# Loading a weight matrix with one 128-partition transfer per slice, three later loads in flight, and a randomly shaken schedule

## Chip, cores, metric

The kernel runs on one core of a Trainium2 chip. The metric is device time in microseconds (us) per execution. The span in a profile, first to last instruction, is 1.7 to 1.9 us shorter than the measured time in nearly all runs. PE is the matmul engine, PEld its weight load, DVE the vector engine, ACT the scalar engine, POOL the general one, and SP the one that mostly issues transfers. ACT issues transfers too. "SPq" and "ACTq" are the instruction queues of SP and ACT. A transfer "lands" at its last completion event.

## The reference

```python
x = A_x                                   # 2048 x 448, bfloat16
xn = layernorm(x)
# branch A: linear attention, 16 heads of 28, feature map softmax(+/- q w_phi)
# branch B: the one that this change touches
h = silu(xn @ B_w1)                       # B_w1: 448 x 1792
branch_B = h @ B_w2                       # B_w2: 1792 x 448
return x + branch_A(xn) + branch_B
```

## The kernel before

The kernel is one program of about 4,900 instructions. A small list scheduler written in Python orders the instructions of each engine before they are emitted. PE's order is fixed by the program text; the scheduler only orders the other engines.

PE works on two halves of its rows at once: partitions 0 to 63 (`LO`) and 64 to 127 (`HI`). The 448 rows of w1 are seven slices `s` of 64 rows. In SBUF, `LO` holds columns 0 to 895 of a slice and `HI` holds columns 896 to 1791 of the same 64 rows. A pair of transfers, one issued by SP and one by ACT, brings in one or two slices. Both sides of each transfer have the 64 rows outermost:

```python
w1v = B_w1.rearrange("(s p) f -> p s f", p=64)
def load_w1(a, b, after=None):
    n = (b - a) * 64 * 896 * 2
    load(w1_sb[LO, a:b, :], w1v[:, a:b, 0:896],    n, 1792, f"w1l{a}", issue=480)
    load(w1_sb[HI, a:b, :], w1v[:, a:b, 896:1792], n, 1792, f"w1h{a}", eng="act", issue=480, after=after)
...
load_x(0, 1); load_x(1, 2)
load_w1(0, 2, after=...); load_w1(2, 4)
load_x(2, 3); load_x(3, 4, eng="act")
load_w1(4, 6); load_w1(6, 7)
```

PE starts with warm-up matmuls, transposes the first normalised tiles of x, and then needs slices 0 and 1, slices 2 and 3, and slices 4 to 6, in that order:

```python
f1a(0, 0, 2)                # tile 0, slices 0 and 1
X_tr(1, ...); X_ev(1, ...)  # transposes on PE, evictions on ACT and DVE
f1a(0, 2, 4); ...; f1a(1, 0, 4)
for h in range(2):          # then slices 4..6
    for s in range(4, NS): ...
```

The later loads (q/k weights, v weights, more of x, w2) each wait for a mark on PE's progress, so that they do not come too early.

The softmax here doesn't subtract the row's maximum and nothing guards it: scores larger than these inputs give would overflow.

Of the kernel before, what the change touches and what calls it, by code (L numbers as in the profile page):

```python
# [138 lines left out]
class _Prog:  # L139
# [56 lines left out]
            return 230.0  # L196
        return 110.0

    def schedule(self, pe0, passes=6):
        ops = self.ops  # L200
        for o in ops:
            for d in o.deps:
                ops[d].users.append(o.id)
            for d in o.odeps:
                assert ops[d].eng == o.eng, "order-only deps must be same-engine"
                ops[d].users.append(o.id)
        t = 0.0
        when = {}
        seen = False
        for o in ops:  # L210
            if o.eng == "pe":
                if o.name != "warm" and not seen:
                    seen = True
                    t = max(t, pe0)
                when[o.id] = t
                t += o.dur
        best = None
        for _ in range(passes):
            order, span = self._pass(when)
            if best is None or span < best[0]:  # L220
                best = (span, order, [(o.start, o.end) for o in ops])
            when = {oid: ops[oid].start for oid in order["pe"]}
        for o, (a, b) in zip(ops, best[2]):
            o.start, o.end = a, b
        self.order = best[1]
        self.makespan = best[0]
        return best[1]

    def _pass(self, when):
        ops = self.ops  # L230
        n = len(ops)
        lat = self.lat
        tend = max(when.values()) + 3000.0
        for o in reversed(ops):
            if o.eng == "pe":
                o.alap = when[o.id]
                continue
            m = tend
            for u in o.users:
                uu = ops[u]  # L240
                if u in o.odeps:
                    continue
                m = min(m, uu.alap - (lat(o, uu) if o.id in uu.deps else 0.0))
            extra = 0.0
            if o.is_dma:
                extra = o.fixed if o.fixed is not None else 1200.0 + o.nbytes
            o.alap = m - o.dur - extra

        ndeps = [len(o.deps) + len(o.odeps) for o in ops]
        ready = {e: set() for e in ENGINES}  # L250
        for o in ops:
            if ndeps[o.id] == 0:
                ready[o.eng].add(o.id)
        eng_free = {"pe": 800.0, "act": 800.0, "dve": 800.0, "pool": 800.0, "sp": 800.0}
        act_table = [None]
        dma_free = [0.0]
        order = {e: [] for e in ENGINES}
        done = 0
        WAIT_TOL = 60.0

        def est(o):
            t = eng_free[o.eng]
            for d in o.deps:
                dd = ops[d]
                t = max(t, dd.end + lat(dd, o))
            for d in o.odeps:
                t = max(t, ops[d].end if not ops[d].is_dma else ops[d].start + ops[d].dur)
            if o.eng == "act" and o.table is not None and act_table[0] is not None and o.table != act_table[0]:
                t += 1300.0
            return t  # L270

        while done < n:
            best = None
            for e in ENGINES:
                if not ready[e]:
                    continue
                c = [(est(ops[i]), ops[i]) for i in ready[e]]
                t0 = min(x[0] for x in c)
                t, o = min(((t, o) for t, o in c if t <= t0 + WAIT_TOL), key=lambda x: (x[1].alap, x[1].id))
                for t2, o2 in c:  # L280
                    if o2 is o or o2.alap >= o.alap or t2 >= t + o.dur:
                        continue
                    la = max(t - o.alap, t + o.dur - o2.alap, 0.0)
                    lb = max(t2 - o2.alap, t2 + o2.dur - o.alap, 0.0)
                    if lb < la - 1.0:
                        t, o = t2, o2
                if best is None or t < best[0]:
                    best = (t, o)
            assert best is not None, "scheduler deadlock"
            t, o = best  # L290
            ready[o.eng].discard(o.id)
            o.start = t
            if o.is_dma:
                issue_end = t + o.dur
                eng_free[o.eng] = issue_end
                if o.fixed is not None:
                    o.end = t + o.fixed
                else:
                    x0 = max(issue_end + 900.0, dma_free[0])
                    dma_free[0] = x0 + o.nbytes  # L300
                    o.end = dma_free[0] + 300.0
            else:
                o.end = t + o.dur
                eng_free[o.eng] = o.end + (0.0 if o.eng == "pe" else 30.0)
                if o.eng == "act" and o.table is not None:
                    act_table[0] = o.table
            order[o.eng].append(o.id)
            done += 1
            for u in o.users:
                ndeps[u] -= 1  # L310
                if ndeps[u] == 0:
                    ready[ops[u].eng].add(u)
        return order, max(o.end for o in ops)


def bass_parallel_sum__linear_kernel_hedgehog__dense_activation_silu__prompt_kernel(
# [16 lines left out]
    NB = 4  # L333
# [4 lines left out]
    with es:  # L338
# [68 lines left out]
        P = _Prog()  # L407
# [79 lines left out]
            load(x_sb[:, t0:t1, :], xv[:, t0:t1, :], (t1 - t0) * 128 * D * 2, (t1 - t0) * D * 2, f"x{t0}", issue=430, after=after,  # L487
                 eng=eng)

        w1v = B_w1.rearrange("(s p) f -> p s f", p=64)  # L490
        def load_w1(a, b, after=None):
            n = (b - a) * 64 * 896 * 2
            load(w1_sb[LO, a:b, :], w1v[:, a:b, 0:896], n, 1792, f"w1l{a}", issue=480)
            load(w1_sb[HI, a:b, :], w1v[:, a:b, 896:1792], n, 1792, f"w1h{a}", eng="act", issue=480, after=after)

        P.op("act", 1, lambda e: e.activation(tabw[:], neghalf[:], ACTF.Silu), [neghalf[:]], [tabw[:]],  # L496
             table="silu", name="tab", ordered=True)
        load_x(0, 1)
        load_x(1, 2)
        load_w1(0, 2, after=P.ops[P.last[("pool", "o")]])  # L500
        load_w1(2, 4)
        load_x(2, 3)
        load_x(3, 4, eng="act")
        load_w1(4, 6)
        load_w1(6, 7)
        P.op("pool", 300, lambda e: e.memset(BD[:], 0.0), [], [BD[:]], name="bd0", ordered=True)
        for p0 in (0, 904):
            P.op("pool", 150, lambda e, p0=p0: e.memset(wraw[:, :, p0:p0 + 8], 0.0), [], [wraw[:, :, p0:p0 + 8]],
# [1 line left out]
        wpv = A_w_phi.rearrange("(k q l) d f -> q l d k f", q=2, l=2)  # L510
        wvv = A_wqkv[:, 2 * D:3 * D].rearrange("(s p) c -> p s c", p=64)

        def load_wqk(after):
            load(wraw[:, 0:2, 8:904], A_wqkv[0:256, 0:896].rearrange("(b p) c -> p b c", p=128), 256 * 896 * 2, 1792, "wqk0",
                 after=after)
            load(wraw[:, 2, 8:904], A_wqkv[256:384, 0:896], 128 * 896 * 2, 1792, "wqk1", after=after)
            load(wraw[LO, 3, 8:904], A_wqkv[384:448, 0:896], 64 * 896 * 2, 1792, "wqk2", after=after)
            for q in range(2):
                for l in range(2):
                    p0 = (64 if q else 8) + l * DH  # L520
                    load(BD[p0:p0 + DH, :, l * DH:(l + 1) * DH], wpv[q, l], DH * NB * DH * 2, DH * 2, f"wphi{q}{l}", issue=430)

        w2v = B_w2.rearrange("(f p) d -> p f d", p=128)
        wov = A_wo.rearrange("(h s e) c -> s h e c", s=NS, e=4)
# [68 lines left out]
        def F1(c, i, j0, nt, mid=None):  # L593
# [3 lines left out]
            for s in range(NS):  # L597
                pair([(bank(2 * sl + q)[:, 0:n], w1_sb[HALF[q], s, i * 128:(i + 1) * 128],
                       xT[HALF[q], c % NXC, s, j0 * 128:j0 * 128 + n], s == 0, s == NS - 1) for q in range(2)], n, "f1")
                if mid is not None and s == 2:  # L600
                    mid()
            src = two(sl)[:, :, 0:n]
            dst = hT[:, c % NH, i:i + FH + 1:FH, j0 * 128:j0 * 128 + n]
# [218 lines left out]
                    F1mm(sa[u // 2], u % 2, u, s, t, 1)  # L822

        f1a(0, 0, 2)
        load_wqk(mark())
        X_tr(1, 3, 0, HS)
        X_ev(1, 3, 0, HS)
        f1a(0, 2, 4)
# [5 lines left out]
        LN_b(2, od=True)  # L834
        LN_b(3, od=True)
        pads_init()
        marks = [mark()]
        f1a(1, 0, 4)
        marks.append(mark())
        P.unit = "F1A"  # L840
        for h in range(2):
            for s in range(4, NS):
                for u in range(2):
                    F1mm(sa[h], u, 2 * h + u, s, 0, 2)
            F1silu(sa[h], 2 * h)
        marks.append(mark())
        sb_ = take()
        for u in range(2):
            P.unit = "F1B%d" % u
# [3 lines left out]
                X_tr(2, 3, 0, NS)  # L853
                X_ev(2, 3, both=True)
        F1silu(sb_, 4)
        marks.append(mark())
        sl = take()
        X_tr(3, sl, 0, NS)
        X_ev(3, sl, both=True)
        give(sl)  # L860
        F1(0, 6, 0, 2)
        marks.append(mark())
        FT_tr(0)
        for i in range(FH):
            F1(0, i, 2, 2)
            marks.append(mark())
            if i == 2:
                FT_tr(1)
            if i in (4, 5, 6):
                FM(i - 4)  # L870
        load(wv_sb[LO], wvv, D * D * 2, D * 2, "wv0", after=marks[2])
        load(wv_sb[HI], wvv, D * D * 2, D * 2, "wv1", after=marks[3])
        load_x(4, 6, after=marks[4])
        load(w2_sb[:, 0:7], w2v[:, 0:7], FF * D, 896, "w2", after=marks[5])
        load_x(6, 8, after=marks[7])
        load(w2_sb[:, 7:14], w2v[:, 7:14], FF * D, 896, "w2", after=marks[8])

        def prep(t):
            LN(t)
            X_dma(t)  # L880
# [188 lines left out]
```

## Time and profile before

| | before |
|---|---|
| median time of the first three runs | 152.81 us (152.14 to 152.93) |
| span of the profiled execution | 151.6 us |
| PE busy | 142.8 us, 94% of the span |
| w1 in all | 1.6 MB, 896 pieces of 1792 bytes |

The first view is part 2 of the page of the kernel before: the span in 40 slices of 3.8 us, busy share in tenths. PEclk is the clock granted to PE (time before the first clock event counts as full), and DMA is the mean busy share of the sixteen DMA engines. Shares of DMA add up packet times, so they can pass 1.

```profile
PE   6769959999999999999999999999999999999990
...
PEclk9959999999999999999999999999999999999999
DMA  3996895093772997239781023333376344863323
```

PE is full from the seventh slice on. Only the first 22 us have gaps, and there the DMA share is 0.84.

The chain of waits of the kernel before, in order of time (start, length, what), shows how small the gaps are:

```profile
2.49 6.10 DMA w_sb<-in_B_w_dram
...
8.73 1.04 PE psum L432 x16
...
12.07 1.81 PE psum L432 x30
...
20.71 1.57 issue
22.28 125.66 PE psum L432 x1774
...
147.96 0.62 DVE x_sb L752
```

From 22.28 us PE works for 125.66 us without a wait, and then the last addition and store follow. The early part is a wait for a w1 transfer. The 30 matmuls at 12.07 us begin with slice 6, the last, whose second half landed at 11.93 us. The piece called "issue" is 1.57 us in which PE stood still.

PE's waits of the kernel before (engine, line, what it waited for: total us, times, longest) name the same two:

```profile
PE psum L432 <- DMA w_sb<-in_B_w_dram: 2.1, 2, 1.3
PE psum L432 <- issue: 1.6, 1, 1.6
```

The DMA view of the kernel before lists the issues (what, queue, how many, KB each, median us from issue to landing). The w_phi load has no landing time. The view takes a landing from sixteen completion events, and the trace has only fifteen for each of these four small transfers of 28 rows:

```profile
w_sb<-in_B_w_dram SPq DMA_DIRECT2D x3, 224.0 KB, 5.4
w_sb<-in_B_w_dram ACTq DMA_DIRECT2D x3, 224.0 KB, 6.1
...
BD<-in_A_w_phi_dram SPq DMA_DIRECT2D x4, 6.1 KB
```

Two lines of PE's timeline before (start, length, what, count, idle before) show the clock. The same 16 matmuls of 128 columns take 0.62 us at full clock and 1.04 us after the second gap:

```profile
6.67 0.62 PE L432 MATMUL psum<-xT,w_sb 64*128 64x128 bf16 x16 [0.74 <-DMA w_sb<-in_B_w_dram]
...
8.73 1.04 PE L432 MATMUL psum<-xT,w_sb 64*128 64x128 bf16 x16 [1.32 <-DMA w_sb<-in_B_w_dram]
```

### The profile page before, as it was taken

To read this page: it belongs to the slowest core of one execution; us is meant where nothing else is said; L and a number is where in the kernel's file an instruction comes from. 1 tells how busy PE (TensorE), PEld (TensorE's weight loads), DVE (VectorE), ACT (ScalarE), POOL (GpSimd) and SP (SyncE) were. 2 spreads that over 40 slices of the span, in tenths; PEclk is the share of its full clock that TensorE was granted. 3 is DMA by queue.
4 is the path that set the end of the run, shared out by engine and by line. 5 is a ranking of instruction groups with operands and counts; after the bars stand their busy time and mean duration, and the time that the engine had idled before them with its cause. 6 is when DMAs were issued, how large, how long until landed. Compare 5 with 4: busy or idle time off the path is not lost.

```text
span 151.6 us, 4915 instructions
## 1 busy us (share of the span) xinstructions
PE 142.8 (94%) x2118; PEld 88.3 (58%) x2118; DVE 96.7 (64%) x179; ACT 84.4 (56%) x106; POOL 83.9 (55%) x95
## 2 busy tenths in 40 slices
PE   6769959999999999999999999999999999999990
PEld 2379957555556555555555556565556666666550
DVE  2747548699998376990129697874047694848633
ACT  3115748988955976895779587678573102011110
POOL 3307000706999996969902899999991402222130
PEclk9959999999999999999999999999999999999999
DMA  3996895093772997239781023333376344863323
GB/s 79 255 272 178 227 316 206 4 169 73 225 93 42 137 173 153 69 97 157 158 183 35 0 63 80 69 74 69 73 107 79 81 123 124 49 191 73 102 84 121
DMA packets 43678, 18.42 MB, mean 122 GB/s; under 512 B 36680, under 2 KB 43400, under 8 KB 43656
## 3 DMA queue, kind: packets, MB, share of 16 engines
q1 hardware_dynamic: 43000, 17.19, 53.6%
q10 hardware_dynamic: 656, 0.92, 2.4%
q8 instruction: 17, 0.28, 0.8%
q14 instruction: 5, 0.04, 0.1%
HBM read 7.48 MB, written 1.84 MB: 61 GB/s over the span
## 4 chain that ended last, share of the span: by engine, by line
PE 91%; DMA 4%; issue 1%; ACT 1%; DVE 0%; DVEq 0%; ACTq 0%
PE psum L432 90%; DMA w_sb<-in_B_w_dram 4%; PE psum L445 1%; ACT L496 1%; DVE x_sb L752 0%; DVEq L1020 0%; ACTq L463 0%
## 5 line engine op out<-in xcount | busy, mean ns | idle before, releaser
L640 POOL TENSOR_TENSOR E<-E,Rk 128x896 bf16<-128x896 bf16 x32 | 53.3, 1699 | 8.7 <-ACT E L450 6.3
L432 PE MATMUL psum<-xT,w_sb 64*128 64x512 bf16 (+2 forms) x522 | 48.1, 331 | 2.1 <-DMA w_sb<-in_B_w_dram 2.1
L432 PE MATMUL psum<-w_sb,hT 64*128 64x448 bf16 x448 | 45.2, 349 | 0.0
L450 ACT ACTIVATE hT<-psum 128x1024 bf16<-128x1024 f32 (+1 forms) x32 | 28.9, 917 | 12.8 <-PE psum L432 12.0
L432 PEld LDWEIGHTS psum<-xT,w_sb 64*128 64x128 bf16 x522 | 26.5, 98 | 15.4 <-DMA w_sb<-in_B_w_dram 1.7
L432 PEld LDWEIGHTS psum<-w_sb,hT 64*128 64x128 bf16 x448 | 24.1, 94 | 16.6
L633 DVE TENSOR_REDUCE Sk<-E 128x64 f32<-128x1792 bf16 x16 | 31.9, 2004 | 2.4 <-ACT E L450 2.3
L450 ACT ACTIVATE E<-psum 128x896 bf16<-128x896 f32 x32 | 27.4, 916 | 6.2 <-PE psum L432 6.0
L450 ACT ACTIVATE xT<-psum 128x448 f32<-128x448 f32 (+2 forms) x12 | 5.7, 481 | 33.8 <-PE psum L432 21.9
L432 PE MATMUL psum<-wqk,xT 64*128 64x448 bf16 x224 | 23.6, 349 | 0.0
L704 POOL TENSOR_TENSOR xT<-xT,x_sb 128x448 f32<-128x448 f32 x8 | 8.3, 1034 | 24.9 <-ACT xT L450 24.9
L432 PEld LDWEIGHTS psum<-wqk,xT 64*128 64x128 bf16 x224 | 12.2, 94 | 8.6
L557 DVE TENSOR_SCALAR xnd<-x_sb,mv,rstd 128x896 bf16<-128x896 bf16 (+2 forms) x18 | 11.1, 656 | 9.1 <-POOL rstd L547 9.1
L547 POOL TENSOR_TENSOR rstd<-ve,neghalf 128x1 f32<-128x1 f32 x16 | 8.8, 564 | 8.7 <-DVE ve L545 8.4
L692 POOL TENSOR_TENSOR Ye<-Ye,x_sb 128x448 f32<-128x448 f32 x8 | 8.2, 1035 | 7.7 <-DVE Ye L690 7.7
L432 PE MATMUL psum<-wv_sb,xT 64*128 64x448 bf16 x112 | 11.9, 349 | 0.0
L539 DVE BATCH_NORM_STATS2 st<-x_sb 128x6 f32<-128x448 bf16 x16 | 9.5, 608 | 3.4 <-DMA x_sb<-in_A_x_dram 3.4
L432 PE MATMUL psum<-wo_sb,E 64*128 64x448 bf16 x112 | 11.3, 349 | 0.0
L690 DVE TENSOR_TENSOR Ye<-psum,Ye 128x448 f32<-128x448 f32 x8 | 5.0, 621 | 9.0 <-ACT Ye L450 8.9
L729 DVE TENSOR_TENSOR E<-psum,rden 128x224 bf16<-128x224 f32 x32 | 10.3, 383 | 0.3
L545 POOL TENSOR_SCALAR ve<-mv 128x1 f32<-128x1 f32 x12 | 2.3, 216 | 12.4 <-DVE mv L543 12.4
L432 PEld LDWEIGHTS psum<-wo_sb,E 64*128 64x128 bf16 x112 | 6.2, 94 | 4.4
(42 smaller groups left out, 102.0 us busy)
## 6 DMA issues: line engine op xcount, KB each, us to landing
out_dram<-x_sb SPq DMA_DIRECT2D x8, 224.0 KB, 2.2
w_sb<-in_B_w_dram SPq DMA_DIRECT2D x2, 784.0 KB, 6.7
x_sb<-in_A_x_dram SPq DMA_DIRECT2D x2, 448.0 KB, 4.5
wv_sb<-in_A_wqkv_dram SPq DMA_DIRECT2D x2, 392.0 KB, 4.7
wo_sb<-in_A_wo_dram SPq DMA_DIRECT2D x14, 56.0 KB, 2.2
w_sb<-in_B_w_dram SPq DMA_DIRECT2D x3, 224.0 KB, 5.4
w_sb<-in_B_w_dram ACTq DMA_DIRECT2D x3, 224.0 KB, 6.1
phT<-in_A_wqkv_dram SPq DMA_DIRECT2D x1, 448.0 KB, 5.6
```

Of the source, the lines that this page charges most:

```text
L432: ins = e.matmul(dst, lhsT, rhs, start=st, stop=sp, skip_group_check=True)
L450: return P.op("act", d_act(n), lambda e: e.activation(dst, src, func, scale=scale), reads=reads or [src], writes=writes or [dst], table=ta ...
L539: P.op("dve", 630, lambda e: e.bn_stats(st6[:, t, :], xs), [xs], [st6[:, t, :]], name="bnst", ordered=od)
L545: lambda e: e.tensor_scalar(ve[:, t:t + 1], mv[:, t, 1:2], EPS_LN, None, ALU.add),
L547: P.op("pool", 580, lambda e: e.tensor_tensor(rstd[:, t:t + 1], ve[:, t:t + 1], neghalf[:], ALU.pow), [ve[:, t:t + 1], neghalf[:]], [rstd[ ...
L557: lambda e, dst=dst, src=src: e.tensor_scalar(dst, src, mv[:, t, 0:1], rstd[:, t:t + 1], ALU.subtract, ALU.mult),
L633: dve(lambda e: e.tensor_reduce(Sk[:, t % 3, :].rearrange("p (h g) -> p h g", g=2), Er, AXL.X, ALU.add), d_dve(1792), [Er], [Sk[:, t % 3, ...
L640: pool(lambda e, Eh=Eh, Rb=Rb: e.tensor_tensor(Eh, Eh, Rb, ALU.mult), 1770, [Eh, Rh], [Eh], "phi%d" % qk)
L690: dve(lambda e: e.tensor_tensor(y, b, y, ALU.add), d_dve(D), [b, y], [y], "ye_d")
L692: pool(lambda e: e.tensor_tensor(y, y, x_sb[:, t, :], ALU.add), 1110, [y, x_sb[:, t, :]], [y], "ye_x")
L704: pool(lambda e: e.tensor_tensor(y, y, x_sb[:, t, :], ALU.add), 1110, [y, x_sb[:, t, :]], [y], "yl_x")
L729: dve(lambda e, dst=dst, src=src, rb=rb: e.tensor_tensor(dst, src, rb, ALU.mult), d_dve(224), [src, r], [dst], "o")
```

## The change

The intent is to bring each w1 slice into all 128 partitions with one transfer, so that a slice is complete sooner and fewer transfers are issued. The later loads no longer wait for PE's progress. Each waits for the load three before it in a chain, and the w2 loads are cut in two. The list scheduler repeats its pass 400 times with random priorities and keeps the order with the shortest modelled time. The last lines of the diff ("early U" in the texts below) insert some matmuls of the attention branch two slices earlier into a late loop of branch B. The core of the diff:

```diff
-        w1v = B_w1.rearrange("(s p) f -> p s f", p=64)
-        def load_w1(a, b, after=None):
-            n = (b - a) * 64 * 896 * 2
-            load(w1_sb[LO, a:b, :], w1v[:, a:b, 0:896], n, 1792, f"w1l{a}", issue=480)
-            load(w1_sb[HI, a:b, :], w1v[:, a:b, 896:1792], n, 1792, f"w1h{a}", eng="act", issue=480, after=after)
+        w1v = B_w1.rearrange("(s p) (h f) -> h p s f", p=64, h=2)
+        chain = []
+        def chained(*args, **kw):
+            chain.append(load(*args, after=chain[-3], **kw))
+        def load_w1(a, b):
+            for s in range(a, b):
+                chain.append(load(w1_sb[:, s, :], w1v[:, :, s, :], 128 * 896 * 2, 1792, f"w1{s}", eng=("sp", "act")[s % 2], issue=480))
...
         load_x(0, 1)
-        load_x(1, 2)
-        load_w1(0, 2, after=P.ops[P.last[("pool", "o")]])
-        load_w1(2, 4)
-        load_x(2, 3)
+        load_x(1, 2, eng="act")
+        load_w1(0, 5)
+        load_x(2, 3, eng="act")
         load_x(3, 4, eng="act")
-        load_w1(4, 6)
-        load_w1(6, 7)
+        load_w1(5, 7)
...  (wqk, wv, x 4..7 and w2 go through chained(); the marks on PE's progress are gone)
-    def schedule(self, pe0, passes=6):
+    def schedule(self, pe0, passes=6, shaken=400):
...
+            if shake > 0 and not o.is_dma:
+                seed = (seed * 1103515245 + 12345) % 2147483648
+                o.alap += (seed / 2147483648.0 - 0.5) * 200.0 * (1 + shake % 5)
...
-                if mid is not None and s == 2:
+                if mid is not None and s == 0:
                     mid()
```

More of the change, by code (lines that the diff above doesn't have):

```diff
@@ L217, in schedule @@
         best = None
-        for _ in range(passes):
-            order, span = self._pass(when)
+        base = when
+        for k in range(passes + shaken):
+            if k == passes:
+                base = {oid: best[2][oid][0] for oid in best[1]["pe"]}
+            order, span = self._pass(base, k - passes + 1)
             if best is None or span < best[0]:
                 best = (span, order, [(o.start, o.end) for o in ops])
-            when = {oid: ops[oid].start for oid in order["pe"]}
+                if k >= passes:
+                    base = {oid: ops[oid].start for oid in order["pe"]}
+            if k < passes:
+                base = {oid: ops[oid].start for oid in order["pe"]}
         for o, (a, b) in zip(ops, best[2]):
@@ L227, in schedule, with _pass @@
         return best[1]
-    def _pass(self, when):
+    def _pass(self, when, shake=0):
         ops = self.ops
@@ L233, in _pass @@
         tend = max(when.values()) + 3000.0
+        seed = 7919 * max(shake, 0) + 17
         for o in reversed(ops):
@@ L511, in bass_parallel_sum__linear_kernel_hedgehog__dense_activation_silu__prompt_kernel, with load_bulk @@
         wvv = A_wqkv[:, 2 * D:3 * D].rearrange("(s p) c -> p s c", p=64)
-        def load_wqk(after):
-            load(wraw[:, 0:2, 8:904], A_wqkv[0:256, 0:896].rearrange("(b p) c -> p b c", p=128), 256 * 896 * 2, 1792, "wqk0",
-                 after=after)
-            load(wraw[:, 2, 8:904], A_wqkv[256:384, 0:896], 128 * 896 * 2, 1792, "wqk1", after=after)
-            load(wraw[LO, 3, 8:904], A_wqkv[384:448, 0:896], 64 * 896 * 2, 1792, "wqk2", after=after)
+        def load_bulk():
+            for b in range(NB):
+                r = 128 if b < 3 else 64
+                chained(wraw[0:r, b, 8:904], A_wqkv[b * 128:b * 128 + r, 0:896], r * 1792, 1792, f"wqk{b}", issue=450)
             for q in range(2):
@@ L521, in load_wqk @@
                     load(BD[p0:p0 + DH, :, l * DH:(l + 1) * DH], wpv[q, l], DH * NB * DH * 2, DH * 2, f"wphi{q}{l}", issue=430)
+            for q in range(2):
+                chained(wv_sb[HALF[q]], wvv, D * D * 2, D * 2, f"wv{q}")
+            chained(x_sb[:, 4:6, :], xv[:, 4:6, :], 256 * D * 2, 4 * D, "x4", issue=430)
+            for a, b in ((0, 4), (4, 7)):
+                chained(w2_sb[:, a:b], w2v[:, a:b], (b - a) * 128 * D * 2, D * 2, "w2", issue=430)
+            chained(x_sb[:, 6:8, :], xv[:, 6:8, :], 256 * D * 2, 4 * D, "x6", issue=430)
+            for a, b in ((7, 11), (11, 14)):
+                chained(w2_sb[:, a:b], w2v[:, a:b], (b - a) * 128 * D * 2, D * 2, "w2", issue=430)
         w2v = B_w2.rearrange("(f p) d -> p f d", p=128)
@@ L824, in bass_parallel_sum__linear_kernel_hedgehog__dense_activation_silu__prompt_kernel @@
         f1a(0, 0, 2)
-        load_wqk(mark())
+        load_bulk()
         X_tr(1, 3, 0, HS)
@@ L836, in bass_parallel_sum__linear_kernel_hedgehog__dense_activation_silu__prompt_kernel @@
         pads_init()
-        marks = [mark()]
         f1a(1, 0, 4)
-        marks.append(mark())
         P.unit = "F1A"
@@ L845, in bass_parallel_sum__linear_kernel_hedgehog__dense_activation_silu__prompt_kernel @@
             F1silu(sa[h], 2 * h)
-        marks.append(mark())
         sb_ = take()
@@ L855, in bass_parallel_sum__linear_kernel_hedgehog__dense_activation_silu__prompt_kernel @@
         F1silu(sb_, 4)
-        marks.append(mark())
         sl = take()
@@ L861, in bass_parallel_sum__linear_kernel_hedgehog__dense_activation_silu__prompt_kernel @@
         F1(0, 6, 0, 2)
-        marks.append(mark())
         FT_tr(0)
@@ L865, in bass_parallel_sum__linear_kernel_hedgehog__dense_activation_silu__prompt_kernel @@
             F1(0, i, 2, 2)
-            marks.append(mark())
             if i == 2:
@@ L870, in bass_parallel_sum__linear_kernel_hedgehog__dense_activation_silu__prompt_kernel @@
                 FM(i - 4)
-        load(wv_sb[LO], wvv, D * D * 2, D * 2, "wv0", after=marks[2])
-        load(wv_sb[HI], wvv, D * D * 2, D * 2, "wv1", after=marks[3])
-        load_x(4, 6, after=marks[4])
-        load(w2_sb[:, 0:7], w2v[:, 0:7], FF * D, 896, "w2", after=marks[5])
-        load_x(6, 8, after=marks[7])
-        load(w2_sb[:, 7:14], w2v[:, 7:14], FF * D, 896, "w2", after=marks[8])
         def prep(t):
```

## The prediction

> **What bounds the kernel now.** PE. The page gives PE 142.8 of 151.6 us busy. In the chain of waits the piece from 22.28 to 147.94 us is unbroken PE work (125.7 us, no wait); the tail (last addition, store) is 3.6 us. So only the first 22 us can give anything. There, by the timeline: PE waits 0.7 us and 1.3 us for w1 slices (until 6.67 and 8.73); the windows view shows a granted clock of 0.59 from 8.73 to 12.07, costing about 1.4 us; the last w1 piece lands at 11.9, just as PE wants it (12.04); and PE stands still from 20.71 to 22.28 ("issue", 1.6 us; a 16 KB instruction packet was still moving until 20.98 through DMA engines that were fully busy). The most that a perfect change could win is about 5 us; a realistic k=16 version of this one would win 1 to 3 us. The random shaking and the earlier insertion of U act where PE already never waits: worth nothing, at most harm.
>
> **What the change does to w1.** Bytes are the same (1.6 MB). Before, each transfer has 64 rows outermost on both sides, and each leaves 16 completion events in the trace. After, the source of a slice is [h=2][p=64][896 elements] and the destination is [128][896]. The Trainium skill (DMA: Bandwidth & Descriptors, "Why a DMA increments its semaphore by 16 and not by 1", on how many engines) says that a transfer is split over the largest k up to 16 that divides the outermost size of both sides. Here that is gcd(2, 128) = 2. This trace agrees with the rule where it can be tested: the four w_phi loads, 28 rows outermost, leave 15 events, as k = 14 plus one made-up remainder would; the others leave 16. So I expect the w1 load on two DMA engines instead of sixteen.
>
> **Cost.** In the trace a 1792-byte packet takes 75 to 79 ns of an engine at its best (and 100 to 120 when all sixteen are saturated). Two engines must each move 7 x 64 = 448 of them: 34 to 35 us, plus about 2.5 us for their share of x and the first wqk pieces, plus 2 us of start and 1 us of landing: slice 6 lands at about 39 to 40 us instead of 11.9. PE's order is fixed by the program, so it cannot work ahead. From the moment slice 6 is there, PE still has 147.96 - 12.07 - 1.57 = 134.3 us to do, about 1.7 us more because its clock will have dropped in the wait, then 3.6 us of tail and 1.2 us between span and measured time: 180 us. The loads chained behind w1 (wqk, wv, w2) start late too, but at 16 engines they should stay ahead of PE.
>
> **Prediction: 179 us.** The chance that the two-engine reading is right I put at about two in three: a tuned kernel's author would have noticed 30 us. If it is wrong, about 150.5 us. So the range has to be wide: 149 to 188. Chances: faster by over 2% 0.13, within 2% 0.21, slower 0.66.
>
> **What would show it.** Right: w1 issue-to-landing of 10 us and more, each w1 transfer with about 3 completion events, DMA share near 2/16 in the first 30 us, PE idle in stretches of about 10 us waiting for w1 by line, then unbroken work. Wrong: sixteen events per slice, slices landing 1 us apart, PE's two early waits shorter, clock at 1.0 from 9 to 12 us, and the 20.7 us gap gone or moved.
>
> **What would make it wrong.** The source's two outer sizes being merged or reordered before they reach the hardware; two engines running faster per packet than 75 ns; a new PE stall later from the shaken order.

## The result

| | before | after |
|---|---|---|
| median time | 152.87 us (152.14 to 152.98, 4 runs) | 178.88 us (178.72 to 179.89, 4 runs) |
| ratio after/before | | 1.171, 95% interval 1.165 to 1.178 |
| span of the profiled execution | 151.6 us | 177.0 us |
| last w1 piece landed | 11.9 us | 37.0 us |
| completion events per w1 transfer | 16 | 3 |
| median length of a 1792-byte packet, whole execution | 79 ns | 74 ns |
| the same, from 1 to 37 us | 100 ns | 74 ns |

Ratios and intervals are from fast runs alone, so they are not quite the ratio of the quoted medians.

The page of the kernel after, part 2 (slices of 4.4 us):

```profile
PE   6403151069999999999999999999999999999991
...
PEclk9965555558999999999999999999999999999999
DMA  2122111256975749039539880052228934383332
```

In the first eight slices PE is mostly idle, and so are the DMA engines: the kernel waits for a load while nearly all of the DMA engines are free. The windows view gives one stretch of that (start:end, length, busy us of PE, PEld, DVE, ACT and POOL, clock, DMA share, GB/s):

```profile
15.00:25.00 10.00, 2.36 (x46) 1.85 (x46) 0.32 (x2) 0.42 (x2) 0.00 (x0) 0.50 0.13 50
```

The DMA share is 0.13, about 2/16, and 50 GB/s are moved. Two engines that take 74 ns for 1792 bytes would move 48 GB/s (an estimate from these packets). Transfers of both SP and ACT were in flight then, so the two queues used the same two engines: spreading the slices over two queues did not spread them over more engines. The x loads show it too. They run on all sixteen, and of the first one behind w1 fourteen events came by 13.4 us and the last two only at 24.8 and 25.1 us. Before, the stretch from 8.04 to 11.45 us moved 269 GB/s.

The chain of waits after has two new pieces: SP's long issue of slice 4, and the 28 us from the start of slice 6's issue (8.9 us of them the issue itself) to its landing. The unbroken PE work that follows is as long as before:

```profile
2.55 6.33 SPq L473
...
8.92 28.12 DMA w_sb<-in_B_w_dram
...
37.08 3.38 PE psum L442 x29
...
47.77 125.63 PE psum L442 x1772
...
173.42 0.62 DVE x_sb L772
```

PE's waits after:

```profile
PE psum L442 <- DMA w_sb<-in_B_w_dram: 16.9, 5, 5.4
PE psum L442 <- ACT xT L460: 8.3, 1, 8.3
```

The first line was expected. The second one (8.3 us) was not: PE waited for ACT to evict the first transposed tile. The DMA view after shows that the w1 transfers have lost their landing time, just as the 28-row loads had none before, and that the three small x loads on ACT took 14.3 us from issue to landing (median):

```profile
w_sb<-in_B_w_dram SPq DMA_DIRECT2D x4, 224.0 KB
...
w_sb<-in_B_w_dram ACTq DMA_DIRECT2D x3, 224.0 KB
...
x_sb<-in_A_x_dram ACTq DMA_DIRECT2D x3, 112.0 KB, 14.3
```

Lines of the timeline after show why ACT was late:

```profile
1.25 16.54 SPq L473 DMA_DIRECT2D w_sb<-in_B_w_dram  x4
...
3.25 9.50 ACTq L473 DMA_DIRECT2D x_sb<-in_A_x_dram  x2
...
13.95 0.60 ACT L460 ACTIVATE xT<-psum 128x256 bf16<-128x256 bf16 x2 [11.66 <-issue]
...
14.48 1.22 PE L442 MATMUL psum<-xT,w_sb 64*128 64x128 bf16 x16 [8.26 <-ACT xT L460]
...
21.33 0.61 PE L442 MATMUL psum<-xT,w_sb 64*128 64x128 bf16 x8 [5.42 <-DMA w_sb<-in_B_w_dram]
...
37.08 3.38 PE L442 MATMUL psum<-xT,w_sb 64*128 64x256 bf16 x30 [1.39 <-DMA w_sb<-in_B_w_dram]
```

Issuing two small x loads occupied ACT's queue from 3.25 to 12.75 us (one of them alone 8.4 us, where 0.3 to 0.6 us is usual). They stood behind w1 slices 1 and 3. In the row of sizes below, the same issue took 9.4, 1.0, 1.0 and 0.6 us with 2, 4, 8 and 16 outermost, so the hold-up goes with the outermost size; how the queue is held, the profile does not show. The issue of slice 5 followed, and ACT's eviction of xT could only run at 13.95 us. SP was held in the same way: its issues of slices 4 and 6 took 6.3 and 8.9 us. This ACT wait did not set the end. PE still had to wait for the later slices, at 21.33 and finally at 37.08 us.

The sum closes: PE starts on slice 6 at 37.1, plus 136.3 us of PE work to 173.4, plus 3.6 us of tail to 177.0, plus 1.7 us between span and time gives the 178.75 us of the profiled execution.

### The profile page after: what moved, and what is told of

It is laid out like the page before. It is cut to its first block, busy times and chain, and to the rows that moved or that the text cites. A ratio compares the mean times of both kernels' runs of the same rounds, so it can differ in the third digit from the quotient of the medians.

```text
span 177.0 us, 4906 instructions
## 1 busy us (share of the span) xinstructions
PE 146.7 (83%) x2118; PEld 89.1 (50%) x2118; DVE 96.9 (55%) x179; ACT 84.4 (48%) x106; POOL 84.2 (48%) x95
## 3 DMA queue, kind: packets, MB, share of 16 engines
q10 hardware_dynamic: 822, 1.03, 1.7%
## 4 chain that ended last, share of the span: by engine, by line
PE 77%; DMA 16%; SPq 4%; DVE 0%; DVEq 0%; issue 0%
PE psum L442 76%; DMA w_sb<-in_B_w_dram 16%; SPq L473 4%; PE psum L455 1%; DVE x_sb L772 0%; DVEq L1027 0%
## 5 line engine op out<-in xcount | busy, mean ns | idle before, releaser
L442 PE MATMUL psum<-xT,w_sb 64*128 64x512 bf16 (+2 forms) x522 | 51.4, 345 | 25.1 <-DMA w_sb<-in_B_w_dram 16.9
L442 PEld LDWEIGHTS psum<-w_sb,hT 64*128 64x128 bf16 x448 | 24.2, 94 | 16.6
L610 DVE COPY xT<-psum 128x448 bf16<-128x448 bf16 (+2 forms) x8 | 2.5, 329 | 30.6 <-PE psum L455 30.1
L442 PEld LDWEIGHTS psum<-wqk,xT 64*128 64x128 bf16 x224 | 12.2, 94 | 8.5
L442 PE MATMUL psum<-wv_sb,xT 64*128 64x448 bf16 x112 | 11.9, 349 | 0.0
```

The source lines that it names most:

```text
L442: ins = e.matmul(dst, lhsT, rhs, start=st, stop=sp, skip_group_check=True)
```

## The experiments

Three theories had to be told apart. **A:** the source's outermost size of 2 confines each w1 transfer to two DMA engines, and that is the whole loss. **B:** a source that walks two dimensions is slow as such, or reading both halves of a DRAM row with one transfer is. **C:** the chained later loads or the shaken order cost a part.

### e1_two_halves: the change without the single transfer

```diff
-                chain.append(load(w1_sb[:, s, :], w1v[:, :, s, :], 128 * 896 * 2, ..., eng=("sp", "act")[s % 2], ...))
+                load(w1_sb[LO, s, :], w1v[0, :, s, :], 64 * 896 * 2, 1792, f"w1l{s}", issue=480)
+                chain.append(load(w1_sb[HI, s, :], w1v[1, :, s, :], 64 * 896 * 2, 1792, f"w1h{s}", eng="act", issue=480))
```

> The changed kernel with only the w1 slices put back into two transfers of 64 rows each (both sides 64 rows outermost, so 16 DMA engines); chain of three, shaking and early U kept. Theory (two DMA engines are the whole loss): 149 to 152.5 us, 16 completion events per w1 transfer, last w1 piece landed by 10 to 12 us. Rival (the later loads chained behind w1, or the shaken order, carry a good part): stays over 156 us.

Measured: 152.86 us (before in the same rounds: 152.90), ratio 1.001, interval 0.995 to 1.006. Each transfer left 16 completion events, and the last piece landed at 11.9 us. All of the loss is gone, and the rest of the change (chain, shaking, early U), taken together, is worth nothing measurable. C falls.

Why did the rest, with its earlier first slices, not win? PE's waits of this run show that the waits for w1 and w2 shrank to 0.7 us in all and another wait came:

```profile
PE psum L442 <- ACT xT L460: 1.5, 1, 1.5
...
PE psum L442 <- DMA w_sb<-in_B_w_dram: 0.7, 2, 0.5
```

Its timeline shows where that wait came from: ACT was issuing loads until 7.05 us and evicted xT only then.

```profile
5.82 1.23 ACTq L473 DMA_DIRECT2D w_sb<-in_B_w_dram  x2
...
7.10 0.60 ACT L460 ACTIVATE xT<-psum 128x256 bf16<-128x256 bf16 x2 [4.80 <-PE psum L455]
...
7.74 1.03 PE L442 MATMUL psum<-xT,w_sb 64*128 64x128 bf16 x16 [1.52 <-ACT xT L460]
...
12.01 1.81 PE L442 MATMUL psum<-xT,w_sb 64*128 64x256 bf16 x30 [0.19 <-DMA w_sb<-in_B_w_dram]
```

The 16 matmuls at 7.74 us took 1.03 us, so PE was at half clock. Its clock events say so too: the first rise to full clock in this run is at 10.47 us. But the late eviction and the cold PE are not what kept the gain away. The last w1 piece landed no sooner (11.88 us against 11.93 before), and PE began the 30 matmuls that start with slice 6 just after it, at 12.01 us against 12.07. The run e3 below, with the loads of the kernel before, settles it: there PE's clock was full from 6.54 us on and ACT's eviction cost PE only 0.4 us, the last piece landed at 11.88 us, and the same group again began at 12.01 us:

```profile
12.01 1.81 PE L442 MATMUL psum<-xT,w_sb 64*128 64x256 bf16 x30 [0.29 <-DMA w_sb<-in_B_w_dram]
```

Here, first slices that landed earlier won nothing, because the last one did not land earlier.

### e2_only_w1: the single transfer without the rest of the change

```diff
         def load_w1(a, b, after=None):
-            n = (b - a) * 64 * 896 * 2
-            load(w1_sb[LO, a:b, :], ...); load(w1_sb[HI, a:b, :], ..., eng="act", after=after)
...  (w1v as in the change)
+            for s in range(a, b):
+                load(w1_sb[:, s, :], w1v[:, :, s, :], 128 * 896 * 2, 1792, f"w1{s}", eng=("sp", "act")[s % 2],
+                     issue=480, after=after if s % 2 else None)
```

> The kernel before with only the w1 loads changed to one transfer of [2][64][896] into 128 partitions per slice; nothing else. Theory: 176 to 183 us, 3 completion events per slice, slice 6 landed at 36 to 39 us. Rival (chain or shaking): within 3 us of 152.9.

Measured: 179.48 us, ratio 1.175 (1.167 to 1.183); 3 events per slice; slice 6 landed at 37.97 us. The chain of waits has the same long piece, followed by the same unbroken work:

```profile
10.32 27.65 DMA w_sb<-in_B_w_dram
...
46.81 127.16 PE psum L432 x1758
```

The one edit alone makes the whole loss.

### d2, d4, d8, d16: the size of the outermost dimension

Their outputs are wrong, which doesn't matter for the times. The changed kernel is kept, and so are the 128 destination partitions, the 1792-byte pieces and their number. Only the source differs: it walks 128 rows of w1 (half of them shared with the next slice), interleaved so that its two dimensions can't merge, with k outermost.

```diff
-    chain.append(load(w1_sb[:, s, :], w1v[:, :, s, :], ...))
+    r0 = 64 * min(s, 5)
+    src = B_w1[r0:r0 + 128, 0:896].rearrange("(a b) f -> b a f", b=K)     # K = 2, 4, 8, 16
+    chain.append(load(w1_sb[:, s, :], src, ...))
```

> Wrong result on purpose: the changed kernel, each w1 transfer still 128 partitions of 1792-byte pieces, but the source walks 128 rows of w1 as [4][32][896] (rows interleaved, so that the two dimensions can't merge). Theory: 4 DMA engines, 5 completion events, 224 packets of about 75 ns each: slice 6 lands near 20 to 21 us, time 160 to 164 us. Rival (a source of two dimensions that steps across rows is slow as such, in DRAM or in issuing): about 179 us as with two.

> Wrong result on purpose: as the run with [4][32][896], but the source is [16][8][896]. Theory: 16 DMA engines, 16 events, slice 6 lands by 10 to 12 us, time 149 to 153 us, like the run with two halves. Rival (two-dimensional source slow as such): about 179 us.

> Wrong result on purpose: as the runs with 4 and 16 outermost, with [8][16][896]. Theory: 9 completion events, 112 packets on each of 8 engines: 8.4 us of packets, slice 6 lands at 11.5 to 13.5 us, time 153 to 156 us.

> Wrong result on purpose, and the control of the row of sizes: [2][64][896] taken from rows instead of column halves. Theory: 3 events, slice 6 lands at 36.5 to 37.5 us, 178 to 180 us as the changed kernel. Rival (what hurts is that both halves of one DRAM row are read by one transfer): clearly faster than 178.

| source | completion events per slice | packets per engine, times 74 ns | slice 6 landed | last slice landed | time |
|---|---|---|---|---|---|
| [2][64] | 3 | 448: 33.2 us | 36.5 us | 36.5 us | 178.18 us |
| [4][32] | 5 | 224: 16.6 us | 21.3 us | 21.3 us | 163.93 us |
| [8][16] | 9 | 112: 8.3 us | 13.1 us | 15.0 us | 156.34 us |
| [16][8] | 16 | 56: 4.1 us | 10.6 us | 11.5 us | 153.71 us |

(Packets per engine are worked out: 7 slices x 128 pieces / k. With 16 the packets were longer, 100 ns in the median up to 12 us, so 4.1 us is too low there.) The record's ratios to the kernel before are 1.168, 1.073, 1.024 and 1.006, with the verdicts slower, slower, unclear (interval 1.019 to 1.030) and same. The events are k + 1 up to 8, and 16 at 16. The extra event does not come with the data: in the changed kernel's slice 0, issued from 1.25 to 1.95 us, one event is at 2.5 us and the two others are at 11.7 and 12.2 us. The time follows the packets per engine. B falls: a two-dimensional source is fast when 16 is outermost, and two halves of the same DRAM row are no slower than two different rows (178.88 against 178.18 us). Sixteen outermost took 0.7 us more than expected (two runs, 152.64 and 154.78 us). With 8, the time missed its expected range by 0.3 us; slice 5, behind x2 and x3 on ACT's queue, landed after slice 6 there, which probably accounts for it. With 4, slice 6 landed 0.3 us later than expected, and the time was in its range.

The DMA view gives the same reading without counting events. With 4 outermost there is no landing time, and with 16 there is:

```profile
w_sb<-in_B_w_dram SPq DMA_DIRECT2D x4, 224.0 KB
```

```profile
w_sb<-in_B_w_dram SPq DMA_DIRECT2D x4, 224.0 KB, 6.0
...
w_sb<-in_B_w_dram ACTq DMA_DIRECT2D x3, 224.0 KB, 6.4
```

### e3_only_shaking and e4_only_chain: the other two parts alone

```diff
# e3: the kernel before, and only this
-    def schedule(self, pe0, passes=6):
+    def schedule(self, pe0, passes=6, shaken=400):     # with the random term in _pass
# e4: the kernel before, and only this
-        load(wv_sb[LO], wvv, ..., after=marks[2]) ...   # marks on PE's progress
+        chained(wv_sb[HALF[q]], wvv, ...) ...           # three in flight; wqk and w2 cut smaller
```

> The kernel before with only the list schedule shaken (400 more passes); loads untouched. Theory (orders on the other engines can't win where PE never waits): within 0.7% of before, 152 to 154 us. Rival (the shaken order wins or loses a part): over 1% away.

> The kernel before with only the later loads chained three deep and cut smaller, in place of the marks on PE's progress. Theory: 151 to 153.5 us; PE's stand-still near 20.7 us (seen in the profile of before, not in the run with two halves) shrinks or is gone. Rival (earlier bulk loads crowd out the last w1 pieces): slower by over 1%.

Measured: shaking alone 152.64 us, ratio 1.001 (0.997 to 1.006); the chain alone 153.30 us, ratio 1.005 (0.999 to 1.010). Neither is a change at 1%. (The early U was not run alone; e1 shows only that the three together change nothing.) In the chain's profile the stand-still near 20.7 us is indeed gone, as expected, but PE still waits 1.5 us for w1 at 8.71 us. The four runs of that kernel have spans from 150.6 to 152.3 us, wider than what is to be explained. In the profile of the shaken order the stand-still is there, but half as long, although no load was changed:

```profile
21.42 0.23 PE L442 MATMUL psum<-BD,phT 64*128 64x56 bf16 x4 [0.76 <-issue]
```

So the stand-still varies without any change to the loads, and its length in one profile proves little.

### c1, c2, c3, c4: tries to beat both

All four start from e1. c1 uses fewer and larger w1 transfers and moves x1 back to SP. c2 puts both first evictions on DVE. c3 is c2 with x2 and x3 issued on SP after all of w1. c4 is c3 with the warm-up matmuls cut in two.

```diff
# c1
+        load_x(1, 2); load_w1(0, 1); load_w1(1, 2); load_w1(2, 4); load_w1(4, 6); load_x(2, 3); load_x(3, 4, eng="act"); load_w1(6, 7)
# c2
-        X_ev(0, 3, 0, HS)
+        X_ev(0, 3, 0, HS, both=True)
# c3, on top of c2
-        load_w1(0, 5); load_x(2, 3, eng="act"); load_x(3, 4, eng="act"); load_w1(5, 7)
+        load_w1(0, 7); load_x(2, 3); load_x(3, 4)
# c4, on top of c3
-        warm(10, d=427.0)     # pairs of 512 columns
+        warm(20, d=213.5)     # pairs of 256 columns
```

> A try to beat both: the run with two halves, but fewer and larger w1 transfers (slices 0, 1, then 2+3, 4+5, 6) and x1 back on SP, so that ACT issues 6 loads instead of 10 and is free for the first eviction of xT. Theory (in the run with two halves the 1.5 us PE wait for ACT xT came from ACT still issuing loads until 7.05 us): that wait is gone or under 0.5 us, span 149 to 150, time 150.5 to 152. Rival (w1 data comes no sooner): same as the run with two halves.

Measured: 153.92 us, ratio 1.010 (1.007 to 1.014): 1% slower. The ACT wait is gone as expected, but the larger transfers land later and PE waits 2.4 us for w1 in three pieces.

> The run with two halves, with one edit: both halves of the first xT eviction go to DVE, so PE's first real matmuls wait for nothing on ACT. Theory: the 1.5 us wait of PE for ACT xT is gone, 151 to 152.3 us. Rival (the next wait, for ACT's second eviction or for w1, takes its place): 152.5 to 153 us.

Measured: 152.84 us median of four, from 151.44 to 154.24: two of the four count as slow. The two fast ones took 151.44 and 151.81 us, less than any of the seven runs of the kernel before in these rounds (152.27 to 152.88), but two runs settle nothing. In the profile of the second the wait for ACT is gone and PE starts at full clock at 6.45 us, but a wait for the last w1 halves comes at 10.81 us:

```profile
6.45 0.62 PE L442 MATMUL psum<-xT,w_sb 64*128 64x128 bf16 x16 [0.41 <-issue]
...
10.81 2.28 PE L442 MATMUL psum<-xT,w_sb 64*128 64x256 bf16 x34 [1.38 <-DMA w_sb<-in_B_w_dram]
```

> The run with both first evictions on DVE, with x2 and x3 issued on SP after all w1 halves, so that the upper halves of slices 5 and 6 are no longer issued last on ACT (they landed at 10.7 and 11.1 us there, and PE waited 1.4 us for them until 10.81). Theory: that wait shrinks below 0.6 us, time 150.3 to 151.6 us in the runs without a late end. Rival (DRAM and DMA engines are the limit, not the order): no change from the run before it.

Measured: 152.83 us, ratio 1.002 (0.997 to 1.007). The w1 wait shrank to 0.4 us as expected; the last piece landed at 10.21 us and PE began slice 6 at 10.34 us, 1.7 us sooner than in the kernel before. But the time did not fall. PE now waits for DVE instead:

```profile
PE psum L442 <- DVE wqk L814: 1.9, 2, 1.2
...
PE psum L455 <- DVE xnd L577: 0.9, 1, 0.9
PE psum L442 <- DMA w_sb<-in_B_w_dram: 0.9, 2, 0.5
```

> As the run with x2 and x3 last, but the ten warm-up pairs of 512 columns cut into twenty of 256: 40 more PE instructions in time that PE only fills. In two of four runs of the version with evictions on DVE the measured time was 2.7 to 3.4 us above the span instead of 1.7; the guess is an instruction fetch that falls at the very end of PE's program. Theory: shifting the fetches by 40 instructions takes the late ends away: all runs 1.7 to 1.9 us above the span. Rival (late ends have another cause): they stay in some runs.

Measured: 152.91 us, ratio 1.002 (0.998 to 1.006). Its six runs are 1.7 to 1.9 us above the span, but so are the six of c3, which lacks the edit. The guess about a late instruction fetch is therefore neither supported nor refuted.

None of the four is shown to beat the kernel before; c2 stays undecided. In the profiles of c1 and c3, an early wait that was taken away was replaced by another.

## Why the prediction was right

- *Two DMA engines instead of sixteen.* Right. There were three completion events per slice, a DMA share of 0.13 with little but w1 moving, and the row of sizes 2, 4, 8, 16. The Trainium skill (DMA: Bandwidth & Descriptors, "Why a DMA increments its semaphore by 16 and not by 1") states the rule; traces agree for outermost sizes 2, 4, 8, 16 and 28. The page says that both sides' outermost sizes count. Here the destination was always 128 partitions in these transfers, so only the source's part is shown.
- *75 to 79 ns a packet, slice 6 at 39 to 40 us.* Right in kind, 2 to 3 us too late. The packets took 74 ns, 33.2 us in all, and everything else (start, x, landing) took 3.9 us, not the 5.5 us allowed for.
- *134.3 us of PE work after it, 1.7 us for the cold clock.* 136.0 predicted, 136.3 measured. The clock stood at half from 10.31 to 41.03 us.
- *1.2 us between span and time.* It was 1.7 us. The 1.2 came from subtracting the profiled execution's span from the median of other runs; the profiled execution itself took 153.31 us. This and the landing error had opposite signs and partly cancelled. Besides, the prediction's own sum ends at 180 us, and it does not say why 179 was stated. So the closeness of 179 to 178.88 us is partly luck. The range, 149 to 188 us, held both readings, so that meeting it says little; the events and the terms of the sum are the test.
- *PE idle in stretches of about 10 us for w1.* Not quite. The longest w1 wait was 5.4 us, because slices from two queues arrive in turns. The longest wait of all was 8.3 us for ACT, whose queue stood behind the slow transfers. The prediction had no such wait in it. It cost nothing in the end because slice 6 set the time.
- *A version on sixteen engines would win 1 to 3 us; shaking is worth nothing.* The second held (ratio 1.001). The first failed: e1 is at 1.001. The estimate counted the early waits and the half clock from 8.73 to 12.07 us as time to be won. But PE could not begin slice 6 before it landed, and in e1 that was still at 11.9 us, a time that the prediction itself quotes.
- *One chance in three that the reading was wrong.* That doubt came from guessing at the author, not from the trace. The 15 events of the 28-row loads were the better evidence.

What stays open: why PE stands still near 20.7 us in some profiles, and what made two runs each of e1 and c2 end 2.3 to 3.4 us after the span instead of 1.7.

## What to carry to other kernels

Before you merge transfers, look at the outermost size on both sides of the access pattern; here it was the DRAM side that mattered. Joining two good halves with a leading dimension of 2 put the load on two of sixteen DMA engines and cost 26 us, and a landing time missing from the DMA view (or k + 1 completion events) was its signature. The slow transfers also held the queue of the engine that issued the next ones, so work of that engine that had nothing to do with the load got late (8.3 us on ACT). In a start-up where several waits follow each other closely, taking one away is worth only the distance to the next one: test the whole start, not one wait.

## What the Trainium skill lacked or had wrong

- DMA: Bandwidth & Descriptors, "Rules for kernel authors": for two transfers to disjoint partition halves it says "Use one 128-partition transfer". It does not warn, in that row, that the joined source may get a leading dimension of 2. Here the joined form took 178.88 us and the two halves (e1) 152.86 us. The warning stands in another row of the same table, about outermost sizes below 16, and that row was right.
- The same page does not say that issuing stalls behind a transfer that runs on few engines. With two engines, issues on SP took 6.3 and 8.9 us and one on ACT 8.4 us, against 0.3 to 0.9 us for the loads of the kernel before in its first 20 us, and ACT's own work waited with them.
- TensorE: Matmul & The Clock Gate, "Why this matters for your kernels": that row asks for no idle gaps over about 3 us between matmul bursts. Shorter gaps were no safeguard here. In the kernel before, PE was busy for 1.97 of 3.41 us and its longest gap there was 1.3 us (partly in the next window), and the clock still fell to half at 8.04 us for 3.41 us. Idle time alone does not decide it either: in d16, PE was busy for 1.89 us from 9.39 to 12.80 us, with a gap of 1.52 us, and the clock stayed full. One difference is that 22 of the 44 PE instructions in the first stretch were transposes and none in the second; no run tests whether that is the cause. The windows view of the kernel before shows both stretches:

```profile
4.63:8.04 3.41, 1.97 (x44) 1.09 (x40) 2.39 (x9) 0.99 (x3) 0.65 (x1) 1.00 1.09 250
8.04:11.45 3.41, 2.72 (x56) 2.75 (x58) 1.42 (x5) 0.33 (x1) 0.21 (x1) 0.50 1.07 269
```

- No page says how to read a profile's clock before its first clock event. In e1 the first event, a rise to full, is at 10.47 us, yet the view used here counts the time before as full and gives 1.0 for the whole span. The 16 matmuls at 7.74 us took 1.03 us against 0.62 us at full clock, so they ran at about half.
